# Tail stores of 64 rows dealt anew over the DMA engines, in the backward pass of a decode block with attention and a gated bilinear layer

## The chip, the core and the metric

The kernel runs on one core of one Trainium2 chip. The metric is device time in microseconds, from runs without the profiler. Beside those runs there is one profiled execution, with every instruction of the five compute engines and of SyncE (SP) and every packet of the DMA rings.

## The reference, cut to what matters

A block for a batch of 2 and one new token: layer norm, attention of 32 query heads on 16 cached key and value heads of 4,096 positions by 128, and a bilinear layer with gate, up and down weights. The kernel returns the output and the gradients for the input, both caches and all five weights, in bfloat16.

```python
def _B_ref(x, w_gate, w_up, w_down):
    g = jnp.einsum("bsd,df->bsf", x, w_gate)
    u = jnp.einsum("bsd,df->bsf", x, w_up)
    h = g * u
    return jnp.einsum("bsf,fd->bsd", h, w_down)

x = A_x
xn = _layernorm(x, axis=-1)
return x + _A_ref(xn, A_k_cache, A_v_cache, A_wq, A_wo) + _B_ref(xn, B_w_gate, B_w_up, B_w_down)
...
_out, _vjp = jax.vjp(_f, A_x, A_k_cache, A_v_cache, A_wq, A_wo, B_w_gate, B_w_up, B_w_down)
_grads = _vjp(grad_out)
```

What matters here are the gradients of `wq` (576 x 4096, out_4), of `w_gate` and of `w_up` (576 x 4608 each, out_6 and out_7). Each is an outer product: the transposed normalised input times a row of gradients, summed over the two batch entries. Of the 576 rows, 512 make four full blocks of 128; the other 64 are the tail. The tail of each matrix is stored in pieces of 64 rows by 512 columns, 64 KB each.

## The kernel before, in words

Nearly all the traffic is caches: 64 loads of 1 MB (key and value heads) and as many 1 MB stores of their gradients, with the weights and their gradients between them, 186 MB in all. Attention goes in 16 steps (8 groups of two key heads, times two batch entries). Nine pieces of the bilinear layer (`mlp(i, ...)`, i = 0 to 8, 512 hidden columns each) and the ends of the eight groups (`group_back(g)`, g = 0 to 7) are woven in.

The order of all work is written by a planner in the kernel, class `Order`, when the program is built. Each piece of work is a generator that yields its needs with their costs (`DVE(0.42)`, `ACQ("tl")`, `DMA("SP", ...)`), and the planner picks by due times (`PR`, `OFF`). What stands between two yields is emitted without a cost of its own. All large transfers are issued by SP on one ring.

Stores go through `put` (L695 to L700): wait for the pieces, issue the DMA on SP, and hand the buffer back once it has landed. The 64-row tails have buffers of their own, `tl` (two of them), and go through `tail_outer` (L818 to L843). The bilinear piece i stores two tails there, w = 0 for `w_gate` and w = 1 for `w_up`; a group stores one, for `wq`. The work of one tail is four matmuls on TensorE per column half (L831), one cast from PSUM to `tl` (`cp`, L470 on ACT or L472 on DVE), and the store (L699).

How a tail is spread over the sixteen DMA engines depends on how its destination is written. As `[64, 512]` it goes to sixteen engines, four rows each. Where the store's index is in `few` (L823), the destination is viewed with a leading dimension of four, `(r q) f -> q r f`, and it goes to four engines, sixteen rows each. Row p of the buffer then belongs to another row of the matrix, so that the weights on TensorE are taken from `xnq`, a copy of the last 64 columns of `xnr` in that order (made once by ACT at L637, in the tile `xi`, which is free by then).

Which tails go to four engines is set by `FEW_M` and `FEW_G` (L802): in bilinear pieces 0 to 4 only w = 1, in 5 to 8 both, and in groups 3 to 7. That is 18 tails on four engines and 8 on sixteen.

Of the kernel before, what the change touches and what calls it, by code (L numbers as in the profile page):

```python
# [13 lines left out]
P = 128  # L14


def view(t, p0, np_, off, dims):

    (pstep, _), *_ = t.ap
    return bass.AP(t.tensor, t.offset + p0 * pstep + off, [[pstep, np_], *[list(d) for d in dims]])  # L20
# [226 lines left out]
def PE(stream, issue=0.0, quad=None, kind="f"):  # L247
    return ("op", "PE", max(CLK * stream, issue) + 0.03, quad, stream, issue, kind)


def DVE(cost):
    return ("op", "DVE", cost)


def ACT(cost):
    return ("op", "ACT", cost)
# [10 lines left out]
def ACQ(tag):  # L267
    return ("acq", tag)


def REL(tag, i):
    return ("rel", tag, i)


def WAIT(*events):
    return ("wait", events)


def SET(event):
    return ("set", event)  # L280


def SPAWN(gen, prio):
    return ("spawn", gen, prio)


def PRIO(prio):
    return ("prio", prio)


def DMA(engine, cost, nbytes, row=8192):
    packet = 0.0364 * row + 8.7
    return ("dma", engine, cost, 0.02 + nbytes / 16e3 * packet / row, packet)
# [61 lines left out]
def kernel(  # L355
# [22 lines left out]
    nc = tc.nc  # L378
# [9 lines left out]
    NG = Hkv // G  # L388
# [8 lines left out]
    NFS = F // FS  # L397
# [61 lines left out]
    def events(n):  # L459
        return [Event() for _ in range(n)]  # L460
# [19 lines left out]
    xnr = const.tile([P, D], BF16, name="xnr")  # L480
    dyr = const.tile([P, D], BF16, name="dyr")

    def filled(name, shape, dtype, value, eng=nc.vector):
        t = const.tile(list(shape), dtype, name=name)
        eng.memset(t[:], value)
        return t
# [12 lines left out]
    xs = filled("xs", [P, 6, 32], BF16, 0.0)  # L499
    xi = const.tile([P, 2, P], BF16, name="xi")  # L500
    nc.vector.memset(xi[0:2], 0.0)
    xnq = xi[:, 0, 0:64]
    Wdy = filled("Wdy", [P, 2, 160], BF16, 0.0)

    for t in (*W_t[0], *W_t[1], *wm_t, *oT_t):
# [95 lines left out]
    def front():  # L601
        xb = xy[:, 0:D]
        yield DMA("ACT", 0.45, 2304, 1152)
        nc.scalar.dma_start(xb, A_x.rearrange("b s d -> (b s) d"))
        nc.scalar.dma_start(xy[:, D:2 * D], grad_out.rearrange("b s d -> (b s) d"))
        yield ("lset", Ein)
        yield ACT(1.5)
        nc.scalar.activation(warm[:], eps_t[0:1], AF.Sqrt)
        yield WAIT(Ein)
        yield DVE(1.0)  # L610
        for k in range(2):
            nc.vector.bn_stats(bst[:, k], xb[:, k * HD2:(k + 1) * HD2])
        nc.vector.bn_aggr(mv[:], bst[:].rearrange("p k s -> p (k s)"))
        yield ACT(0.3)
        nc.scalar.activation(rstd[:], mv[:, 1:2], AF.Sqrt, bias=eps_t[:], scale=1.0)
        yield DVE(0.6)
        nc.vector.reciprocal(rstd[:], rstd[:])
        nc.vector.tensor_scalar(xnb[:], xb, mv[:, 0:1], rstd[:], op0=ALU.subtract, op1=ALU.mult)
        yield ACT(1.5)
        nc.scalar.activation(warm[:], eps_t[0:1], AF.Exp)  # L620

        yield DVE(0.12)
        nc.vector.tensor_copy(view(xi[:], 0, 2, 0, [[P + 1, 2], [2, 64]]), view(xnb[:], 0, 2, 512, [[0, 2], [1, 64]]))
        i = yield ACQ("m")
        tp = m_t[i][:].bitcast(BF16)
        yield PE(0.02, 0.16)
        for c in range(4):
            nc.tensor.transpose(tp[:, 2 * c:2 * c + 2], xnb[:, c * P:(c + 1) * P], ident[0:2, 0:2])
        for h in range(2):
            nc.tensor.transpose(tp[:, 8 + 2 * h:10 + 2 * h], xi[0:2, h], ident[0:2, 0:2])  # L630
        yield DVE(0.16)
        nc.vector.tensor_copy(xs[:, :, 0:2], tp[:, 0:12].rearrange("p (c b) -> p c b", b=2))
        yield REL("m", i)
        yield SET(Exn)
        yield WAIT(Edy)
        yield from widen(xnb, xnr)
        nc.scalar.copy(xnq.rearrange("p (q r) -> p q r", q=4), xnr[:, 512:576].rearrange("p (r q) -> p q r", q=4))  # L637
        yield SET(Exr)

        yield PRIO(PR["const"])  # L640
        yield WAIT(Econst)
        nr = gg[0:2, 0, 0:4]
        yield DVE(0.3)
        nc.vector.memset(gg[:, 1], 0.0)
        nc.vector.tensor_scalar(nmu[:], mv[:, 0:1], -1.0, None, op0=ALU.mult)
        nc.vector.tensor_scalar(nr[:, 0:2], identf[0:2, 0:2], nmu[:], None, op0=ALU.mult)
        nc.vector.tensor_scalar(nr[:, 2:4], identf[0:2, 0:2], rstd[:], None, op0=ALU.mult)
        i = yield ACQ("m")
        tp, bp = m_t[i], m_t[i][:, 64:68]
        yield PE(0.0, 0.3)  # L650
        for a in range(4):
            for c in range(4):
                nc.tensor.matmul(tp[32 * c:32 * c + 32, 2 * a:2 * a + 2], lhsT=xb[:, P * c + 32 * a:P * c + 32 * a + 32],
                                 rhs=ident[0:2, 0:2], start=True, stop=True)
        for a in range(4):
            nc.tensor.matmul(tp[0:16, 8 + 2 * a:10 + 2 * a], lhsT=xb[:, 512 + 16 * a:528 + 16 * a],
                             rhs=ident[0:2, 0:2], start=True, stop=True)
        nc.tensor.matmul(bp, lhsT=view(ones[:], 0, 2, 0, [[0, P]]), rhs=nr, start=True, stop=True)
        yield DVE(0.9)
        nc.vector.tensor_copy(xnT[:, 0:8], tp[:, 0:8])  # L660
        nc.vector.tensor_copy(xnT[0:16, 8:16], tp[0:16, 8:16])
        nc.vector.tensor_copy(nrT[:], bp)
        for k, op in ((0, ALU.add), (2, ALU.mult)):
            nc.vector.tensor_tensor(xnT[:], xnT[:], view(nrT[:], 0, P, k, [[0, 8], [1, 2]]), op)
        nc.vector.memset(gg[:, 0], 0.0)
        yield REL("m", i)
        yield SET(Eprep)
# [131 lines left out]
                               out_4[0:512, gs[0] * FS:(gs[-1] + 1) * FS], p, E), p)  # L799
        yield SPAWN(release("Q", [grp[g]["Q"] for g in gs], [E]), p)  # L800

    FEW_M, FEW_G = (5, 6, 7, 8), range(3, NG)  # L802
    BUNCH = ((0, 1, 2, 3), (4, 5, 6, 7), (8,))
    Ds, dE = {}, [events(3) for _ in range(NFS)]

# [9 lines left out]
                yield SPAWN(cols_outer(rhss[0], dst, p, E[w]), p)  # L815
        yield SPAWN(release("D", [Ds[k] for k in ks], [*E, *[e for k in ks for e in dE[k][1:]]]), p)

    def tail_outer(rhss, dsts, p, event, w0=0, few=()):  # L818
        i = yield ACQ("tl")
        st = tl_t[i]  # L820
        nw, done = len(rhss), events(2)
        src = [st[64 * w:64 * w + 64, 0:FS] for w in range(w0, w0 + nw)]
        dsts = [d.rearrange("(r q) f -> q r f", q=4) if k in few else d for k, d in enumerate(dsts)]  # L823
        yield SPAWN(put(dsts, src, 64 * FS * 2, 1024, "tl", i, done), p + PR["store"])

        def mk(A):
            def mms(o):
                for w, rhs in enumerate(rhss, w0):
                    for aa in range(2):
                        a = 2 * A + aa  # L830
                        nc.tensor.matmul(o[64 * w:64 * w + 64, aa, 0:P],  # L831
                                         lhsT=(xnq[32 * a:32 * a + 32, :] if w - w0 in few else
                                               xnr[32 * a:32 * a + 32, 512:576]),
                                         rhs=rhs(a), start=True, stop=True)

            def ev(e, o):
                r = slice(64 * w0, 64 * (w0 + nw))
                cp(e, st[r, 256 * A:256 * A + 256].rearrange("p (a f) -> p a f", a=2), o[r, :, 0:P])
            return mms, (0.053, 0.104), 256, ev
        for A in range(2):  # L840
            yield SPAWN(unit(*mk(A), done[A]), p)
        yield WAIT(*done)
        yield SET(event)  # L843
# [12 lines left out]
    def mlp(i, hh, sl, Lgu, Ld, wd_slot):  # L856
# [12 lines left out]
        for w in range(2):  # L869
            for dc in range(5):  # L870
                for a in range(4):
                    if dc < 4:
                        k, rhs = dc, main[w][:, width * dc + FS * hh + P * a:width * dc + FS * hh + P * (a + 1)]
                    else:
                        h, big, c = at[a]
                        k, rhs = 4 + h, T[:, FT * w + c:FT * w + c + P] if big else gu[:, FS * w + c:FS * w + c + P]
# [16 lines left out]
        for k in range(NB):  # L893
            for e in range(2):
                nc.tensor.matmul(  # L895
                    dh, lhsT=Wdy[:, e, 2 * k:2 * k + P], rhs=view(X[:], 0, P, 64 * k + e, [[D, FC], [2, 32]]),
# [14 lines left out]
        po = pr("mlp", MLP_AT[i] / 4) + PR["wout"]  # L911
        yield SPAWN(rows_outer(hb[:], out_8[f0:f0 + FS, :], po, E[0]), po)
        yield SPAWN(tail_outer([lambda a, w=w: D2[32 * a:32 * a + 32, w, :] for w in range(2)],
                               [out[512:576, f0:f0 + FS] for out in (out_6, out_7)], po, dE[i][1],
                               few=(0, 1) if i in FEW_M else (1,)), po)
        for ks in BUNCH:
            if i == ks[-1]:
                yield SPAWN(grads(ks, po), po)
# [38 lines left out]
        for a in range(0, 4, n):  # L957
            _, big, c = at[a]
            t, step = (T, FT) if big else (gu, FS)
# [92 lines left out]
    def group_back(g):  # L1052
# [4 lines left out]
        r = yield ACQ("R")  # L1057
# [8 lines left out]
        for t, x in ((0, R), (1, Q)):  # L1066
# [4 lines left out]
        po = pr("back", 2 * g) + PR["wout"]  # L1071
# [1 line left out]
        t32(rT[:].rearrange("p c m -> p (c m)"), view(R[:], 0, P, 0, [[1, 4], [4, 32]]))  # L1073
        yield SPAWN(rows_outer(R[:], out_5[n0:n0 + FS, :], po, E[0]), po)
        yield SPAWN(tail_outer([lambda a: Q[32 * a:32 * a + 32, :]], [out_4[512:576, n0:n0 + FS]], po, E[1], g % 2,
                               few=(0,) if g in FEW_G else ()), po)
        if g == NG - 1:
            e = Event()
            yield SPAWN(cols_outer(lambda a: Q[32 * a:32 * a + 32, :], out_4[0:512, n0:n0 + FS], po, e), po)
# [20 lines left out]
        for be in range(4):  # L1100
            nc.tensor.matmul(view(rp, 0, P, 2 * be, [[8, GH], [1, 2]]),
                             lhsT=sel[:, be].rearrange("p a i -> p (a i)"), rhs=oT[:, 1, :, 0:2],
# [499 lines left out]
```

## Time and profile before

| | |
|---|---|
| median of 3 runs | 463.68 us (462.95 to 464.49) |
| the profiled execution's own time | 462.65 us |
| its span, first to last instruction | 460.7 us |
| mean granted TensorE clock | 0.721 |
| busy: PE, DVE, ACT, POOL | 80%, 79%, 73%, 31% |
| DMA packets and bytes | 40,494 and 185.97 MB, 404 GB/s |
| tail stores | 26 of 64 KB, issued from 47.1 to 451.3 us |

The span is the time between the first and the last instruction of the execution; the time of the execution has 1.95 us more around it. Busy time is an average over the whole span. In the slices of the page each digit is the busy share of one fortieth of the span, in tenths; the row for DMA is the mean of the sixteen engines. The packet records hold one line for each packet, with its start, length, bytes and ring. A DMA on one engine is a row of data packets and one 4-byte write that counts up the semaphore.

### The profile page before, as it was taken

To read this page: it belongs to the slowest core of one execution; us is meant where nothing else is said; L and a number is where in the kernel's file an instruction comes from. 1 tells how busy PE (TensorE), PEld (TensorE's weight loads), DVE (VectorE), ACT (ScalarE), POOL (GpSimd) and SP (SyncE) were. 2 spreads that over 40 slices of the span, in tenths; PEclk is the share of its full clock that TensorE was granted. 3 is DMA by queue.
4 is the path that set the end of the run, shared out by engine and by line. 5 is a ranking of instruction groups with operands and counts; after the bars stand their busy time and mean duration, and the time that the engine had idled before them with its cause. 6 is when DMAs were issued, how large, how long until landed. Compare 5 with 4: busy or idle time off the path is not lost.

```text
span 460.7 us, 15711 instructions
## 1 busy us (share of the span) xinstructions
PE 369.5 (80%) x6750; PEld 214.3 (47%) x6750; DVE 365.9 (79%) x708; ACT 336.8 (73%) x516; POOL 143.4 (31%) x174
## 2 busy tenths in 40 slices
PE   1688879798986786896978897877988887987994
PEld 1445456555443343554546364544444542544453
DVE  8887888896789687878887679886976987887782
ACT  4269638878986586775767859867867997897973
POOL 0740043403407341660016151050164364063000
PEclk9967676888776667757685678877567676675856
DMA  8999999999999999999999999999999999999995
GB/s 316 413 408 422 410 423 400 410 415 398 373 424 421 408 422 410 421 419 413 413 403 417 417 418 419 422 418 388 398 423 417 418 423 426 423 409 392 421 346 209
DMA packets 40494, 185.97 MB, mean 404 GB/s; under 512 B 3424, under 2 KB 12136, under 8 KB 24040
## 3 DMA queue, kind: packets, MB, share of 16 engines
q1 hardware_dynamic: 40416, 184.96, 99.0%
q8 instruction: 53, 0.87, 0.7%
q14 instruction: 17, 0.14, 0.1%
q10 hardware_dynamic: 8, 0.00, 0.0%
HBM read 92.48 MB, written 92.48 MB: 401 GB/s over the span
## 4 chain that ended last, share of the span: by engine, by line
DMA 34%; PE 30%; ACT 14%; DVE 12%; issue 5%; SPq 3%; DVEq 0%; ACTq 0%
DMA big<-in_A_v_cache_dram 15%; DMA out_dram<-big 14%; ACT big L470 12%; DVE big L466 7%; PE ps_o L1299 5%; PE ps_m L1451 4%; PE ps_o L730 4%; PE ps_m L1277 4%; DMA big<-in_A_k_cache_dram 3%; SPq L1201 2%; PE ps_o L767 2%; DVE big L472 2%; PE ps_m L895 2%; PE ps_m L681 2%; DMA ww<-in_A_wq_dram 1%
## 5 line engine op out<-in xcount | busy, mean ns | idle before, releaser
L470 ACT CAST big<-ps_o 128x1024 bf16<-128x1024 f32 (+2 forms) x309 | 278.9, 964 | 49.8 <-PE ps_o L1299 24.3
L466 DVE STREAM_TRANSPOSE big<-big 128x1024 f32<-128x1024 f32 x146 | 176.3, 1222 | 16.1 <-DMA big<-in_A_v_cache_dram 6.3
L1265 POOL TENSOR_TENSOR BD<-vr,mask 128x2048 bf16<-128x2048 bf16 x32 | 115.3, 3604 | 114.3 <-DVE vr L472 45.4
L472 DVE CAST big<-ps_o 128x1024 bf16<-128x1024 f32 (+1 forms) x69 | 73.4, 1065 | 19.4 <-PE ps_o L767 6.1
L1277 PE MATMUL ps_m<-big,W 128*32 128x128 bf16 x2048 | 59.7, 280 | 4.5 <-issue 1.7
L1242 POOL COPY W<-rep 32x16 bf16<-32x16 bf16 x128 | 24.8, 193 | 117.9 <-DVE rep L1015 102.0
L1277 PEld LDWEIGHTS <-W 128*32 128x32 bf16 x2048 | 47.2, 125 | 25.1 <-issue 23.9
L1299 PE MATMUL ps_o<-BD,dd 32*128 32x512 bf16 x256 | 46.9, 497 | 9.1 <-ACT big L470 8.1
L1299 PE MATMUL ps_o<-BD,pp 32*128 32x512 bf16 x256 | 44.6, 473 | 8.9 <-ACT big L470 7.3
L466 DVE STREAM_TRANSPOSE big<-ww 128x1152 f32<-128x1152 f32 (+1 forms) x25 | 32.9, 1318 | 2.6 <-DMA out_dram<-big 2.5
L1451 PE MATMUL ps_m<-big,pp 128*32 128x512 bf16 x256 | 28.9, 540 | 4.1 <-DVE pp L466 2.4
L1451 PE MATMUL ps_m<-big,dd 128*32 128x512 bf16 x256 | 27.8, 528 | 1.7 <-DVE dd L466 0.6
L1299 PEld LDWEIGHTS <-dd 32*128 32x128 bf16 x256 | 11.2, 98 | 26.5 <-issue 20.0
L1299 PEld LDWEIGHTS <-pp 32*128 32x128 bf16 x256 | 10.3, 95 | 28.1 <-issue 24.5
L767 PEld LDWEIGHTS <-xnr 32*128 32x128 bf16 x368 | 13.1, 114 | 14.5 <-issue 13.1
L730 PE MATMUL ps_o<-dyr,R 32*32 32x288 bf16 x256 | 17.8, 401 | 1.2 <-ACT big L470 1.1
L767 PE MATMUL ps_o<-D,xnr 32*128 32x128 bf16 x256 | 13.9, 265 | 5.7 <-ACT big L470 4.3
L730 PE MATMUL ps_o<-dyr,hb 32*32 32x288 bf16 x288 | 15.7, 328 | 2.8 <-ACT big L470 2.7
L1047 POOL COPY qr<-qd 128x256 bf16<-128x256 bf16 x8 | 3.2, 398 | 47.4 <-DVE qd L472 43.2
L895 PE MATMUL ps_m<-big,Wdy 128*128 128x128 bf16 x162 | 16.7, 285 | 0.6 <-DVE cr L1403 0.5
L895 PEld LDWEIGHTS <-Wdy 128*128 128x128 bf16 x162 | 15.1, 131 | 2.9 <-issue 2.7
L1352 ACT COPY mr<-m 1x128 f32<-1x128 f32 x16 | 4.7, 295 | 15.1 <-DVE m L1350 14.9
(210 smaller groups left out, 488.2 us busy)
## 6 DMA issues: line engine op xcount, KB each, us to landing
out_dram<-big SPq DMA_DIRECT2D x74, 1024.0 KB
big<-in_A_k_cache_dram SPq DMA_DIRECT2D x32, 1024.0 KB
big<-in_A_v_cache_dram SPq DMA_DIRECT2D x32, 1024.0 KB
out_dram<-big SPq DMA_DIRECT2D x17, 576.0 KB
ww<-in_B_w_down_dram SPq DMA_DIRECT2D x9, 576.0 KB
ww<-in_A_wo_dram SPq DMA_DIRECT2D x8, 576.0 KB
ww<-in_A_wq_dram SPq DMA_DIRECT2D x8, 512.0 KB
big<-in_B_w_gate_dram SPq DMA_DIRECT2D x4, 1024.0 KB
```

Of the source, the lines that this page charges most:

```text
L466: nc.vector.transpose(out, in_)
L470: nc.scalar.copy(out, in_)
L472: nc.vector.tensor_copy(out=out, in_=in_)
L681: nc.tensor.matmul(dp[32 * q:32 * q + 32, 0:P], lhsT=W, rhs=view(X, 0, P, xoff(q, s), [[FS, 4], [2, 32]]), start=(s == 0), stop=(s == S - 1))
L730: nc.tensor.matmul(o[32 * q:32 * q + 32, aa, 0:HD2], lhsT=view(t, 32 * q, 32, 2 * A + aa, [[4, 32]]), rhs=dyr[32 * q:32 * q + 32, k * HD2: ...
L767: nc.tensor.matmul(o[:, aa, j * P:(j + 1) * P], lhsT=xnr[32 * a:32 * a + 32, dc * P:(dc + 1) * P], rhs=rhs(a), start=True, stop=True)
L895: nc.tensor.matmul(dh, lhsT=Wdy[:, e, 2 * k:2 * k + P], rhs=view(X[:], 0, P, 64 * k + e, [[D, FC], [2, 32]]), start=(k == 0 and e == 0), s ...
L1242: nc.gpsimd.tensor_copy(view(W_t[t][w][:], 32 * a, 32, 6 + 8 * a, [[G * WW, 4], [WW, G], [1, 2]]), view(rep_t[grp[g]["qs"]][:], 32 * a, 32 ...
L1265: nc.gpsimd.tensor_tensor(BD_t[i][:], view(vr_t[v][:], 0, P, 0, [[0, 16], [1, Dh]]), view(mask16[:], 0, P, 0, [[1, 16], [0, Dh]]), ALU.mult)
L1277: nc.tensor.matmul(sc[32 * cq:32 * cq + 32, :], lhsT=view(W[:], 0, P, (be * G + l) * WW + 6 - 4 * c2 - 2 * l, [[1, 32]]), rhs=view(X[:], 0 ...
L1299: nc.tensor.matmul(o[:, k, :], lhsT=pr2[32 * c4:32 * c4 + 32, :], rhs=BD[32 * c4:32 * c4 + 32, 8 * l + 4 * h2:8 * l + 4 * h2 + 4, :], star ...
L1451: nc.tensor.matmul(ct[32 * j:32 * j + 32, :], lhsT=view(rT, 0, P, 4 * c + 2 * l, [[1, 32]]), rhs=kv_t[kvS[s][t][l]][:, Dh * c:Dh * (c + 4) ...
```

## The change

`few` is now a table from the store's index to the number of engines, four or two. Two permuted copies of the 64 columns are made in `xi` instead of one: the second takes the other half of row 0 of the tile, and one more copy on ACT. The tables deal the tails anew:

- from four engines to two: w = 1 of pieces 0, 1, 2 and 3, w = 0 of piece 8, and the tail of group 7 (six);
- from sixteen engines to four: w = 0 of piece 4, and the tails of groups 1 and 2 (three).

After it 5 tails go to sixteen engines, 15 to four and 6 to two. On every engine the instructions stand in the same order as before.

```diff
-    xnq = xi[:, 0, 0:64]
+    xnq = {4: xi[:, 0, 0:64], 2: xi[:, 0, 64:P]}
...
-        nc.scalar.copy(xnq.rearrange("p (q r) -> p q r", q=4), xnr[:, 512:576].rearrange("p (r q) -> p q r", q=4))
+        for q, t in xnq.items():
+            nc.scalar.copy(t.rearrange("p (q r) -> p q r", q=q), xnr[:, 512:576].rearrange("p (r q) -> p q r", q=q))
...
-    FEW_M, FEW_G = (5, 6, 7, 8), range(3, NG)
+    FEW_M = {0: {1: 2}, 1: {1: 2}, 2: {1: 2}, 3: {1: 2}, **{i: {0: 4, 1: 4} for i in range(4, NFS - 1)}, NFS - 1: {0: 2, 1: 4}}
+    FEW_G = {0: 0, **{g: 4 for g in range(1, NG - 1)}, NG - 1: 2}
...
-        dsts = [d.rearrange("(r q) f -> q r f", q=4) if k in few else d for k, d in enumerate(dsts)]
+        dsts = [d.rearrange("(r q) f -> q r f", q=few[k]) if k in few else d for k, d in enumerate(dsts)]
...
-                                         lhsT=(xnq[32 * a:32 * a + 32, :] if w - w0 in few else
+                                         lhsT=(xnq[few[w - w0]][32 * a:32 * a + 32, :] if w - w0 in few else
...
-                               few=(0, 1) if i in FEW_M else (1,)), po)
+                               few=FEW_M[i]), po)
...
-                               few=(0,) if g in FEW_G else ()), po)
+                               few={0: FEW_G[g]} if FEW_G[g] else {}), po)
```

More of the change, by code (lines that the diff above doesn't have):

```diff
@@ L816, in grads, with tail_outer @@
         yield SPAWN(release("D", [Ds[k] for k in ks], [*E, *[e for k in ks for e in dE[k][1:]]]), p)
-    def tail_outer(rhss, dsts, p, event, w0=0, few=()):
+    def tail_outer(rhss, dsts, p, event, w0=0, few={}):
         i = yield ACQ("tl")
```

## The prediction

> **What bounds the kernel now.** I read the page's slices and queue table first, then the instructions on tile `tl`, then SP's waits and the end of its timeline, and last the single packet records of the trace.
>
> ```profile
> DMA  8999999999999999999999999999999999999995
> ...
> DMA packets 40494, 185.97 MB, mean 404 GB/s; under 512 B 3424, under 2 KB 12136, under 8 KB 24040
> ...
> q1 hardware_dynamic: 40416, 184.96, 99.0%
> ```
>
> The sixteen DMA engines are busy in every slice but the last, and one ring (q1, SP's) holds 99.0% of their time; no compute engine is above 80%. The bound is DMA engine time. SP itself waits 86.7 us for ACT and 63.9 us for DVE, but ahead of a full ring.
>
> The small packets tell the dealing. 201 transfers run on all sixteen engines, each engine closing with one 4-byte semaphore write: 3,216. The tail stores add 18 x 4 + 8 x 16 = 200, the two small output stores 2 x 2, the two small loads on ACT's ring as much: 3,424, the page's count. So a `q=4` tail does run on four engines. After the change it should be 3,424 - 200 + (5 x 16 + 15 x 4 + 6 x 2) = 3,376.
>
> ```profile
> L699 SPq DMA_DIRECT2D out_dram<-tl x26: 472/558/3377, 47.1 to 451.3; - x26
> L470 ACT CAST tl<-ps_o x25: 353/370/440, 46.6 to 450.9; 128x256 bf16<-128x256 f32 x13, 64x256 bf16<-64x256 f32 x12
> ```
>
> Twenty-six tail stores; SP spends about half a microsecond on each.
>
> A mean over engines hides the question, which is who finishes last. The packet records carry start, length, bytes and ring, no engine number; but on one engine the next packet starts 3 to 4 ns before the last one ends, so chains can be followed. A run of sixteen 1,024-byte packets and a semaphore write is a four-engine tail on one of its engines. When the four engines enter it (us from the span's start):
>
> ```
> tail store of      four engines enter it at         last behind first
> mlp 0              52.08   52.12   52.74   53.67     1.6
> mlp 3              112.68  113.05  113.38  116.59    3.9
> mlp 4              224.84  224.92  225.35  230.06    5.2
> mlp 6, first       281.86  281.94  282.30  287.10    5.2
> group 5            361.51  361.63  364.21  367.29    5.8
> group 6            405.41  405.69  408.56  411.77    6.4
> mlp 8, first       440.93  441.81  443.07  446.30    5.4
> ```
>
> So the four are far from alike. One, call it X, is always last. Which is it? The small output store of two rows goes to two engines; its rows start at 451.37 and 452.06, while X ends the transfer before it at 455.95. X is not one of those two.
>
> ```profile
> 449.70 0.27 SPq L1495 DMA_DIRECT2D out_dram<-xy  x1
> 450.85 0.35 SPq L699 DMA_DIRECT2D out_dram<-big  x1
> 451.31 1.08 SPq L699 DMA_DIRECT2D out_dram<-tl  x1
> 453.47 0.38 SPq L699 DMA_DIRECT2D out_dram<-big  x1
> 456.59 0.26 SPq L1495 DMA_DIRECT2D out_dram<-xy  x1
> ```
>
> This is the end of SP's queue. The ring runs on after it: the last packet is X's, at 459.40 of the 460.7 span. The two engines of the small store are A (unimportant: it leads and runs dry after 444) and B, whose chain from the tail at 443.07 to the row at 452.06 has no gap; B is through with the last big store at 455.55, 3.85 us before X. One more laggard, Y, belongs to the twelve engines without tails: it leaves the row store before mlp 8's tail at 448.15 (X 446.30, all others by 443.15) and ends at 459.03, 0.37 before X. On X each transfer was issued 1.4 to 15.9 us before its turn, so X works without a pause; its own work is the span.
>
> No record here names an engine. The Trainium skill ("DMA: Bandwidth & Descriptors", section on why a DMA increments its semaphore by 16) says that a DMA from SP runs on the lowest-numbered k engines, k being the largest number up to 16 that divides both outer dimensions; by that A and B are engines 0 and 1, and X is 2 or 3.
>
> **The change, part by part.** Prices, from the same chains: sixteen packets and the semaphore write, entry to entry, 0.684 us; four, 0.176; thirty-two (read from the 1,024-byte column stores at the end), 1.361.
>
> - Six tails from four engines to two (mlp 0 to 3, one of mlp 8's, group 7): A and B each +1.361 - 0.684 = +0.677, six times +4.06. X and its neighbour each lose 0.684, six times -4.10.
> - Three tails from sixteen to four (group 1, mlp 4's first, group 2): A, B, X and its neighbour +0.684 - 0.176 = +0.508, three times +1.52; the twelve others -0.176, three times -0.53.
> - Net: A and B +5.59 (2.71 of it before 117 us, 1.35 after 440), X and its neighbour -2.58, Y and the rest -0.53.
> - One more copy on ACT, 128x64, at the start: 0.25 us as the one at 10.92, and ACT then sits idle 0.70 until 11.87. Covered; uncovered it would cost 0.25 once.
> - The order of instructions on all five queues is the same in both kernels; the matmuls of nine tails merely take their weights from another place. No wait is added.
> - SP's issue of a two-engine tail is not shown. The row of all tails gives 0.47 to 0.76 us for nearly every one, so 0 to +0.3 each; with 1.4 us of queue ahead at the worst, hidden, hence 0.
>
> Each engine runs at its own pace, so the end is the latest of four sums (packet end in this profile):
> X 459.40 - 2.58 = 456.8. Y 459.03 - 0.53 = 458.5. A would be near 458.6. B: 455.55 + 5.59 = 461.1, less what it spends waiting anyway. It does so once: between 117.3 and 119.6 the 4,096-byte packets of a store issued late show 305 ns instead of 159, since the ring is being filled while they run. The four-engine tail before it was left at 113.36 to 114.07; two stores of 2.49 would end at 118.3 to 119.0, the first engines end at 119.36. So 0.3 to 1.0 us of B's first +2.71 falls into that hole. I take 0.7 (B is one of three close engines): B ends at 460.45, **1.05 us after X did**.
>
> The profiled execution took 462.65 us (span 460.7, 1.95 around it); the sum gives 463.7. The median of the three runs is 463.68, 1.03 above the profiled one; with the same 1.05 added it becomes **464.7 us**. A measurement of this kernel can tell about 0.3% (1.4 us) from no change, so the likeliest is a change inside that bound, on the slow side.
>
> **Rivals.**
>
> *B's lead is smaller than in this profile: slower.* B's lead over X is 1.6 at 52 us and only 3.2 at 443; every engine meets stalls of its own (packets of 700 to 1,200 ns where 309 is usual, and instruction fetches of 0.65 us, X's every 73 us). The change takes 5.59 + 2.58 = 8.2 us from a lead of at most 5.4. With no hole at 117 and one more 0.9 us stall on B the end is 459.40 + (5.59 - 3.85) + 0.9, that is 2.6 us later: 466.3. It decides once B is held over 0.4 us more than I take. For it: even here B comes out last. The Trainium skill's rules for kernel authors (same page, "Rules for kernel authors", use all 16 engines) speak against the change too: an outer dimension below 16 confines the whole DMA to that many engines. By that rule alone, with no lead to eat up, all 5.59 us would be added: 469.3. The table above speaks against that full sum.
>
> *X alone holds the kernel: faster.* If in most runs X is a microsecond further behind (the median is 1.03 above this execution) and B as far ahead as A, X's 2.58 us come off whole: 461.1. For it: X is last of its four in every row. Against it: Y ends only 0.37 us before X and gains 0.53, so in this execution nothing better than 0.9 is open.
>
> *Y is last, and B stays clear: no change that can be told.* Y's 458.5 is 0.9 before the old end: 462.8.
>
> *The two-dimensional store does not land on two engines, or not on those of the small store.* Then six of the moves fall elsewhere; against it stands the count 3,424 that works out exactly, so I give it no share of its own.
>
> **How the numbers follow.** B last but within the bound 0.30, Y last 0.12: together same 0.42. B last by more than the bound: 0.40, because two of the three unknowns (the hole, a stall on B) push that way. X alone: faster 0.18. The range for 8 in 10 runs from a little above the faster rival's 461.1, 462.2, to the slower rival's end, 466.4. Within the forecast alone (0.3 to 1.0 us for the hole) it is 464.4 to 465.1.
>
> **What would show it.** The count of packets under 512 B at 3,376 (packets in all 40,446). Six tails with thirty-two 1,024-byte packets in a row, 1.36 us, on two engines each, the two that also carry the rows of the small store. X and B about level at mlp 6's first tail, where X is 4.8 us behind now, and B the last of the four from about 320 us on. The last packet of the execution on B, some 1 us later than 459.40. I am wrong if the last packet is X's or Y's, if q1's queue runs dry for long stretches (then the order of transfers moved, not only their dealing), or if B's extra packets vanish in pauses that I have not seen.

## The result, and the profile after

The changed kernel takes 467.16 us (median of 5 runs, 465.76 to 468.34), the kernel before 463.80 us (5 runs, 462.95 to 464.49): a ratio of 1.0071, with a 95% interval of 1.0046 to 1.0097. It is slower by 3.3 us (2.1 to 4.5). The forecast was 464.7, with a range up to 466.4; the time lies above it.

The profiled execution of the changed kernel took 467.67 us, 5.0 more than that of before. These are two single executions, one 0.5 above the median of its kernel and one 1.15 below: 1.7 of the 5.0 is the choice of executions.

The page of the changed kernel, its slices and queue table:

```profile
DMA  8999999999999999999999999999999999999995
...
DMA packets 40446, 185.97 MB, mean 399 GB/s; under 512 B 3376, under 2 KB 12088, under 8 KB 23992
...
q1 hardware_dynamic: 40368, 184.96, 98.7%
```

The dealing is what the diff says: 3,376 small packets and 40,446 in all, both as worked out ahead. The engines are busy in the same slices as before, and at first sight nothing is lost. The instructions on tile `tl`:

```profile
L700 SPq DMA_DIRECT2D out_dram<-tl x26: 482/564/2838, 48.0 to 456.0; - x26
L470 ACT CAST tl<-ps_o x25: 357/372/445, 47.4 to 455.4; 128x256 bf16<-128x256 f32 x13, 64x256 bf16<-64x256 f32 x12
```

SP's issues and ACT's casts cost what they did (median 564 ns against 558, 372 against 370); the last tail is merely issued 4.7 us later. The end of SP's queue:

```profile
453.86 0.27 SPq L1497 DMA_DIRECT2D out_dram<-xy  x1
455.24 0.35 SPq L700 DMA_DIRECT2D out_dram<-big  x1
456.03 0.71 SPq L700 DMA_DIRECT2D out_dram<-tl  x1
458.76 0.39 SPq L700 DMA_DIRECT2D out_dram<-big  x1
461.73 0.26 SPq L1497 DMA_DIRECT2D out_dram<-xy  x1
```

The issue at the head of this list stood at 449.70 before, the one at its end at 456.59: SP itself is 4 to 5 us late. Behind it the ring ends on B. From the packet records of the changed kernel (us from the span's start):

```
B   row of the small store            460.30
B   group 7's tail, 32 packets        461.75 to 463.12
B   last big store, 32 packets        463.11 to 464.48
B   row of the last small store       464.48 to 464.53   the last packet
Y   ends                              462.58
A   row of the small store            457.60
most engines leave the last 1 MB store at 456.6 to 457.4; before, at 451.4 to 452.0
```

So B is last, as forecast, with two-engine tail, big store and row in one unbroken chain. But Y, which has three tails less, also ends 3.55 us later than its 459.03 of before, and so do the engines that are never last. Where did the others lose it? Three stretches of the execution (length; busy time of PE, PEld, DVE, ACT and POOL; then the clock, the DMA share and GB/s), first before, then changed:

```profile
120.00:230.00 110.00, 88.30 (x1562) 49.71 (x1551) 88.73 (x161) 78.65 (x120) 37.22 (x50) 0.70 1.02 414
230.00:260.00 30.00, 24.94 (x521) 15.57 (x519) 25.26 (x47) 22.32 (x33) 9.15 (x11) 0.68 1.02 411
260.00:440.00 180.00, 151.94 (x2617) 83.58 (x2615) 142.36 (x254) 145.55 (x221) 60.63 (x65) 0.71 1.01 415
```

```profile
120.00:230.00 110.00, 87.34 (x1602) 48.87 (x1595) 88.97 (x160) 80.91 (x123) 38.44 (x51) 0.72 1.01 411
230.00:260.00 30.00, 21.33 (x482) 13.96 (x484) 22.35 (x43) 18.71 (x29) 9.14 (x11) 0.66 1.00 380
260.00:440.00 180.00, 154.59 (x2580) 82.35 (x2578) 142.61 (x255) 145.55 (x219) 60.56 (x65) 0.69 1.01 412
```

The DMA share hides it; the GB/s show it. Between 230 and 260 us the changed kernel moves 380 instead of 411: 0.9 MB less, or 2.3 us at that rate. The stretch ahead of it lacks 0.8 us and the one behind it 1.3. This is rough, since the stretches stand still while the work moves by up to 5 us. SP's queue at that place, before and changed:

```profile
222.80 2.07 SPq L699 DMA_DIRECT2D out_dram<-tl  x2
...
234.27 1.20 SPq L1194 DMA_DIRECT2D big<-in_B_w_up_dram  x1
235.57 6.81 SPq L1152 DMA_DIRECT2D big<-in_A_k_cache_dram  x2
242.47 0.52 SPq L1179 DMA_DIRECT2D ww<-in_A_wo_dram  x1
```

```profile
224.88 4.75 SPq L700 DMA_DIRECT2D out_dram<-tl  x2
...
238.53 1.15 SPq L1196 DMA_DIRECT2D big<-in_B_w_up_dram  x1
239.77 7.37 SPq L1154 DMA_DIRECT2D big<-in_A_k_cache_dram  x2
247.23 0.38 SPq L1181 DMA_DIRECT2D ww<-in_A_wo_dram  x1
```

The issue of mlp 5's two tails, at 224.88, is 2.1 us later than before and takes 4.75 us, from the start of the first to the end of the second, instead of 2.07: this is the larger step. The two key loads keep SP for 7.37 us instead of 6.81, where an issue normally takes 0.3 to 0.6. They start 4.2 us later, and 4 to 5 us late the stream stays to the end. All sixteen engines added up, from the packet records:

```
us, summed over 16 engines                before   changed
16 x end of the last packet                7350      7432
packets at their usual length (1)          6996      6996
what packets took beyond it                 167       227
instruction fetches                          59        61
no packet recorded                          128       148
(1) 309 ns for 8,192 bytes, 178 for 4,608, 46 for 1,024, and so on, each less
    the 3 to 4 ns by which packets of one engine overlap
```

The work is the same to the last microsecond. The 82 us more (16 x 5.1) are packets that took longer (60) and pauses (20). Fourteen of the engines had less to do than before, and ended late all the same.

### The profile page after: what moved, and what is told of

The parts are those of the page before. It is cut to its first block, busy times and chain, and to the rows that moved or that the text cites. A ratio compares the mean times of both kernels' runs of the same rounds, so it can differ in the third digit from the quotient of the medians.

```text
span 465.9 us, 15712 instructions
## 1 busy us (share of the span) xinstructions
PE 372.5 (80%) x6750; PEld 212.3 (46%) x6750; DVE 366.0 (79%) x708; ACT 337.4 (72%) x517; POOL 143.1 (31%) x174
## 2 busy tenths in 40 slices
DMA packets 40446, 185.97 MB, mean 399 GB/s; under 512 B 3376, under 2 KB 12088, under 8 KB 23992
## 5 line engine op out<-in xcount | busy, mean ns | idle before, releaser
L1279 PE MATMUL ps_m<-big,W 128*32 128x128 bf16 x2048 | 57.5, 273 | 3.2 <-issue 1.0
L1279 PEld LDWEIGHTS <-W 128*32 128x32 bf16 x2048 | 45.7, 122 | 23.7 <-issue 22.5
L1301 PE MATMUL ps_o<-BD,pp 32*128 32x512 bf16 x256 | 46.5, 483 | 7.9 <-ACT big L470 6.5
L1453 PE MATMUL ps_m<-big,dd 128*32 128x512 bf16 x256 | 28.9, 546 | 2.5 <-DVE dd L466 1.9
L897 PEld LDWEIGHTS <-Wdy 128*128 128x128 bf16 x162 | 14.1, 125 | 3.3 <-issue 3.0
```

The source lines that it names most:

```text
L897: nc.tensor.matmul(dh, lhsT=Wdy[:, e, 2 * k:2 * k + P], rhs=view(X[:], 0, P, 64 * k + e, [[D, FC], [2, 32]]), start=(k == 0 and e == 0), s ...
L1279: nc.tensor.matmul(sc[32 * cq:32 * cq + 32, :], lhsT=view(W[:], 0, P, (be * G + l) * WW + 6 - 4 * c2 - 2 * l, [[1, 32]]), rhs=view(X[:], 0 ...
L1301: nc.tensor.matmul(o[:, k, :], lhsT=pr2[32 * c4:32 * c4 + 32, :], rhs=BD[32 * c4:32 * c4 + 32, 8 * l + 4 * h2:8 * l + 4 * h2 + 4, :], star ...
L1453: nc.tensor.matmul(ct[32 * j:32 * j + 32, :], lhsT=view(rT, 0, P, 4 * c + 2 * l, [[1, 32]]), rhs=kv_t[kvS[s][t][l]][:, Dh * c:Dh * (c + 4) ...
```

## The experiments

Each kernel is the changed one with other tables `FEW_M` and `FEW_G` (the engines per tail), so each carries the second copy on ACT. The diffs are cut to these tables; a minus line is the old dealing, as in the first kernel, and in the last one the line of the changed kernel. Ratios are to the kernel before, with 95% intervals; the us behind a ratio are what it adds to 463.6. A sum "with 4.55 in hand" is the prediction's: X ends at 459.40, Y at 459.03, B at 455.55 - 0.7, plus what is dealt to each. "In hand" is what B can take before it ends last.

**The copy alone** (old dealing).

```diff
+    FEW_M = {i: {0: 4, 1: 4} if i > 4 else {1: 4} for i in range(NFS)}
+    FEW_G = {g: 4 if g > 2 else 0 for g in range(NG)}
```

> The tails are dealt as before; only the second permuted copy on ACT is there. Every theory: 463.8 us, within 0.3% of before, since ACT sat idle 0.70 us behind that copy. If it is slower by 1 us or more, the copy at the start moves the whole order of arrivals, and what the changed kernel lost is not due to the dealing.

463.42 us, ratio 1.0010 (0.9997 to 1.0023): the copy costs nothing that can be told. This run gives something else besides, a second execution with the old dealing to look into. Its small store's rows start at 451.21 and 452.81, the last packet ends at 459.28. With 0.05 for the row, 1.41 for the row store, 0.69 for the tail and 1.36 for the big store B would have been through at 456.3: **3.0 us in hand, where the execution of the prediction had 3.85.**

**The four early moves from four engines to two.**

```diff
-    FEW_M = {i: {0: 4, 1: 4} if i > 4 else {1: 4} for i in range(NFS)}
+    FEW_M = {i: {0: 4, 1: 4} if i > 4 else {1: 2 if i < 4 else 4} for i in range(NFS)}
```

> Only the four early moves from four engines to two (mlp 0 to 3). Theory 1, the prediction's sum with B's whole lead of 3.85 us: B 455.55 + 2.71 - 0.7 = 457.6, X 456.7, Y stays at 459.03, so 0.4 us less than before, 463.4 us, same. Theory 2, no lead counts and what is dealt to the two engines is paid in full: +2.7, 466.5 us. Theory 3, B's lead counts only where the work is added: at mlp 3 the two engines are 3.2 to 3.5 us ahead of X, three moves (2.03) and a stall use that up, and the fourth (0.68) is paid: +0 to +0.7, 463.8 to 464.5 us, and B, not X, is the last of the four from mlp 4 on.

464.14 us, 1.0022 (1.0009 to 1.0034): +1.0 us. Neither the sum with all of B's lead (-0.4) nor the full price (+2.7); theory 3 (0 to +0.7) comes nearest. In its trace B ends at 461.67, 0.3 before the last.

**The three moves from sixteen to four.**

```diff
-    FEW_M = {i: {0: 4, 1: 4} if i > 4 else {1: 4} for i in range(NFS)}
-    FEW_G = {g: 4 if g > 2 else 0 for g in range(NG)}
+    FEW_M = {i: {0: 4, 1: 4} if i > 3 else {1: 4} for i in range(NFS)}
+    FEW_G = {g: 4 if g > 0 else 0 for g in range(NG)}
```

> Only the three moves from sixteen engines to four (groups 1 and 2, mlp 4's first). X is last of its four and takes 3 x 0.508 = 1.52 us more, the twelve others 0.53 less. Theories 1 to 3 alike: X ends at 460.9, +1.5, 465.3 us. If the time stays at 463.8, the lag of X is made up elsewhere (its stalls, or waits that it would have had anyway).

465.71 us, 1.0061 (1.0044 to 1.0078): +2.8 us, or 2.4 by the medians, with X last at 462.17. More than the 1.5 of the packets.

**The two late moves from four to two.**

```diff
-    FEW_M = {i: {0: 4, 1: 4} if i > 4 else {1: 4} for i in range(NFS)}
-    FEW_G = {g: 4 if g > 2 else 0 for g in range(NG)}
+    FEW_M = {i: {0: 2 if i == NFS - 1 else 4, 1: 4} if i > 4 else {1: 4} for i in range(NFS)}
+    FEW_G = {g: (2 if g == NG - 1 else 4) if g > 2 else 0 for g in range(NG)}
```

> Only the two late moves from four engines to two (mlp 8's first tail and group 7's). Theory 1 and theory 3: B 455.55 + 1.35 = 456.9, X 458.0, Y 459.03, so 0.4 us less, 463.4 us, same. Theory 2 (paid in full): +1.35, 465.2 us.

463.12 us, 0.9993 (0.9980 to 1.0006): no difference. 1.35 us more on B cost nothing, so some lead there is.

**Which of the three moves?** First mlp 4's alone, then those of groups 1 and 2 alone.

```diff
+    FEW_M = {i: {0: 4, 1: 4} if i > 3 else {1: 4} for i in range(NFS)}     # first kernel
+    FEW_G = {g: 4 if g > 0 else 0 for g in range(NG)}                      # second kernel
```

> Only one of the three moves from sixteen engines to four: mlp 4's first tail, which then stands in a bunch of four four-engine tails (217 to 225 us). Theory P (X, the last of the four, paces the ring, and each such move costs its 0.508 us, or somewhat more, wherever it is): +0.5 to +0.9, about 464.1 us. Theory Q (the bunch is what costs: SP is held longer at the end of it, 6.7 instead of 5.6 us at the next key load, and the other engines run short of work): nearly all of the three moves' +2.4 is here, 465 us or more.

464.60 us, 1.0022 (1.0007 to 1.0036): +1.0 us.

> Only the other two moves from sixteen engines to four: the tails of groups 1 and 2, each alone in its stretch. Theory P: +1.0 to +1.7, about 464.8 us. Theory Q: +1.0 at the most, and no longer hold of SP at 235 us than before.

464.74 us, 1.0018 (1.0006 to 1.0029): +0.8 us. There is no single costly place (theory Q falls): SP's first load at the place named there takes 5.63 us with mlp 4's move alone and 5.60 with the other two, as before. Together the parts come to 1.8, near the packets' 1.5.

**The reverse: mlp 5's tails on sixteen, and all tails on sixteen.**

```diff
+    FEW_M = {i: {} if i == 5 else {0: 4, 1: 4} if i > 4 else {1: 4} for i in range(NFS)}   # mlp 5
+    FEW_M, FEW_G = {i: {} for i in range(NFS)}, {g: 0 for g in range(NG)}                  # all
```

> The reverse, on the kernel before: both tails of mlp 5 go from four engines to sixteen. X has 1.02 us less, the twelve others 0.35 more. By the engines' sums alone Y ends at 459.38 and X at 458.4, no gain, 463.4 us. Theory P (the pacing engine's work counts, about once and a half): -0.4 to -1.5. Theory Q: -1 or better, with SP held less than 5.6 us at the key load behind.

463.22 us, 0.9992 (0.9972 to 1.0011): no gain, as the engines' sums say, since Y then is last.

> All 26 tails on sixteen engines: X and its neighbours have 18 x 0.508 = 9.1 us less, the twelve others, Y among them, 3.17 more. By the sums Y ends at 459.03 + 3.17 = 462.2: +2.8, 466.2 us. If the lag of the last engine is what costs, whichever engine it is, and the lag of Y behind the rest of the twelve is smaller than X's was, less than that: 463 to 465 us. A faster kernel here would mean that the dealing on four engines is itself what costs.

466.58 us, 1.0062 (1.0044 to 1.0079): +2.9 us, where the sum for Y says +2.8. The page counts what that dealing must give, 3,424 + 18 x 12 = 3,640 small packets:

```profile
DMA packets 40710, 185.97 MB, mean 401 GB/s; under 512 B 3640, under 2 KB 12352, under 8 KB 24256
```

Relieving four engines by 9.1 us is worth nothing while one of the twelve others has 3.2 more. The Trainium skill ("DMA: Bandwidth & Descriptors", section "Rules for kernel authors") asks for transfers that use all 16 engines; here the runs decide against it for these 64-row stores, in this order of the other transfers.

**All six moves to two engines, none of the three.**

```diff
+    FEW_M = {i: {0: 2 if i == NFS - 1 else 4, 1: 4} if i > 4 else {1: 2 if i < 4 else 4} for i in range(NFS)}
+    FEW_G = {g: (2 if g == NG - 1 else 4) if g > 2 else 0 for g in range(NG)}
```

> All six moves of the change from four engines to two, none of the three from sixteen to four. The two engines have 4.06 us more, X and its neighbour 4.10 less. Theory S (the prediction's sum: B may take 3.85 + 0.7 = 4.55 us before it shows): Y stays last, -0.4 us, 463.3. Theory L (B has only some 2.3 us in hand, which is what the changed kernel's +3.3 says: 5.59 - 3.3): +1.8, 465.4. Theory A (each part costs what it cost alone, 1.0 for the early four and -0.3 for the late two): +0.7, 464.3. With no lead: +4.1, 467.7.

464.29 us, 1.0020 (1.0006 to 1.0033): +0.9 us (0.3 to 1.5). Its trace shows B last. SP's final issue stands at 457.94:

```profile
455.02 0.39 SPq L700 DMA_DIRECT2D out_dram<-big  x1
457.94 0.26 SPq L1497 DMA_DIRECT2D out_dram<-xy  x1
```

A's row of that store starts at 458.67, at once; B's at 460.62, and that is the last packet (460.68). So the step "Y is last" is wrong here: B is. Against B in the kernel with the copy alone (when B leaves the row store ahead of the tail, us):

```
                      copy alone   six moves   later by   dealt until then
ahead of mlp 4          225.96      229.88       3.92        2.71
ahead of mlp 7          307.13      311.17       4.04        2.71
group 6                 408.68      411.98       3.30        2.71
ahead of mlp 8          443.81      446.49       2.68        2.71
end (first worked out)  456.3       460.68       4.4         4.06
```

B's extra time is what was dealt to it, and up to 1.3 us more that comes and goes. Nothing of it was absorbed at 117 us. With the copy alone, the two nearly equal engines of which B is one leave mlp 3's tail at 115.12 and 115.15 and the two stores behind it at 120.10 and 120.13: 4.98 us, the time of two stores without a slow packet. With the six moves B leaves that tail at 117.69 and the two stores at 122.67: again 4.98. In neither trace is there a hole that B could have filled.

**Six moves again, but all after 280 us.**

```diff
+    FEW_M = {i: {0: 2 if i > 5 else 4, 1: 2 if i in (6, 7) else 4} if i > 4 else {1: 4} for i in range(NFS)}
+    FEW_G = {g: (2 if g == NG - 1 else 4) if g > 2 else 0 for g in range(NG)}
```

> Six moves from four engines to two again, but all after 280 us: both tails of mlp 6 and 7, mlp 8's first and group 7's. The sums of every engine are those of the six of the change. Theory S: -0.4, 463.3 us. Theory L: +1.8, 465.4. If the place counts (a lead is there late and not early, since late moves alone cost nothing): 463.3 to 463.7, clearly below the six of the change.

465.59 us, 1.0035 (1.0019 to 1.0052): +1.6 us. Late moves are no cheaper than early ones (1.6 against 0.9, with intervals that overlap), so the place isn't the reason. In hand were 4.06 - 1.6 = 2.4 us.

**All 18 four-engine tails to two.**

```diff
+    FEW_M = {i: {0: 2, 1: 2} if i > 4 else {1: 2} for i in range(NFS)}
+    FEW_G = {g: 2 if g > 2 else 0 for g in range(NG)}
```

> A large dose: all 18 tails that run on four engines go to two. The two engines have 18 x 0.677 = 12.2 us more, and so must be last. What is missing from 12.2 is what B has in hand. Theory S: 12.2 - 4.55 = +7.6, 471.3 us. Theory L: +9.9, 473.5. With no lead: +12.2, 475.8. More than 12.2: the stores on two engines cost something besides their packets (SP's issue, buffers held longer).

474.27 us, 1.0225 (1.0207 to 1.0243): +10.4 us (9.6 to 11.3), so 1.8 in hand (0.9 to 2.6). The prediction's 4.55 is excluded, for stores that cost their packets and nothing else. B ends last at 471.92, A at 471.42. Now the page shows idle engines too, the q1 share falling from 99.0% and single slices to 8:

```profile
DMA  8999999999999999999999998989999999999985
...
q1 hardware_dynamic: 40380, 184.96, 97.5%
```

**A try at a faster kernel**: the two late moves, and mlp 5's tails on sixteen.

```diff
+    FEW_M = {i: {} if i == 5 else {0: 2 if i == NFS - 1 else 4, 1: 4} if i > 4 else {1: 4} for i in range(NFS)}
+    FEW_G = {g: (2 if g == NG - 1 else 4) if g > 2 else 0 for g in range(NG)}
```

> A try at a faster kernel: the two late moves from four to two, and mlp 5's tails from four to sixteen. X has 1.37 + 1.02 = 2.39 us less, B 1.35 - 1.02 = 0.33 more, Y and the other eleven 0.35 more. By the sums Y is last at 459.38: no change, 463.6 us. If each part brings what it brought alone (-0.3 and -0.4): 462.9.

463.62 us, 1.0005 (0.9990 to 1.0021): no change, as the sums say. With X, Y and B within four microseconds of each other, no dealing tried here beats the kernel before.

**Does a move from sixteen to four cost more than its packets?** The three had cost 2.4 to 2.8 for 1.5, and on top of the six again 3.3 - 0.9 = 2.4.

```diff
+    FEW_M, FEW_G = {i: {0: 4, 1: 4} for i in range(NFS)}, {g: 4 for g in range(NG)}              # all 26 on four
+    FEW_M = {i: {0: 2 if i == NFS - 1 else 4, 1: 2 if i < 4 else 4} for i in range(NFS)}         # and the six on two
+    FEW_G = {g: 2 if g == NG - 1 else 4 for g in range(NG)}
```

> All eight tails that run on sixteen engines go to four (26 on four): X, its neighbour and the two lowest have 8 x 0.508 = 4.06 us more, the other twelve 1.41 less. Theory S (packets only, and X is last): +4.1, 467.7 us. Theory R (a move from sixteen to four costs about 1.6 times its packets, as the three seem to: +2.4 for 1.52): +6.5, 470.1 us.

468.19 us, 1.0094 (1.0068 to 1.0119): +4.4 us (3.2 to 5.5). The packets' 4.1 fits; 1.6 times that is excluded.

> The changed kernel with the other five sixteen-engine tails on four as well: the two lowest engines have 4.06 + 4.06 = 8.1 us more, X and its neighbour as much as before, the twelve others 1.41 less. With 2.4 us in hand for B, as the six late moves and the large dose show: Theory S +5.7, 469.3 us. Theory R: six moves alone +0.9, and 6.5 for the eight: +7.4, 471.0 us.

469.13 us, 1.0119 (1.0090 to 1.0148): +5.5 us (4.2 to 6.9); 8.1 less 2.4 in hand is 5.7. B is last again, at 466.82.

**The eight on eight engines.**

```diff
-    xnq = {4: xi[:, 0, 0:64], 2: xi[:, 0, 64:P]}
+    xnq = {4: xi[:, 0, 0:64], 8: xi[:, 0, 64:P]}
...
+    FEW_M = {i: {0: 4 if i > 4 else 8, 1: 4} for i in range(NFS)}
+    FEW_G = {g: 4 if g > 2 else 8 for g in range(NG)}
```

> The eight tails on sixteen engines go to eight: eight packets and a semaphore write (0.346 us, from 16 x 0.0424 = 0.678 and 4 x 0.0424 = 0.170 about halfway) for 0.176 on eight engines, X among them: 8 x 0.17 = +1.4 us; the other eight have 1.4 less. Theory S: X last, +1.4, 465.0 us. Theory R: +2.2, 465.8.

466.26 us, 1.0049 (1.0027 to 1.0071): +2.3 us (1.3 to 3.3). It tells nothing apart: 1.4 and 2.2 both lie inside.

The sums against the runs, in us against the kernel before:

```
kernel                         last by the sum    4.55 in hand   2.4 in hand   measured
changed kernel                 B                      +1.05          +3.2      +3.3 (2.1 to 4.5)
early four to two              Y; B                   -0.4           +0.3      +1.0 (0.4 to 1.6)
late two to two                Y                      -0.4           -0.4      -0.3 (-0.9 to 0.3)
six to two                     Y; B                   -0.4           +1.7      +0.9 (0.3 to 1.5)
six to two, late               Y; B                   -0.4           +1.7      +1.6 (0.9 to 2.4)
18 to two                      B                      +7.6           +9.8     +10.4 (9.6 to 11.3)
six to two, eight to four      B                      +3.6           +5.7      +5.5 (4.2 to 6.9)
three to four                  X                      +1.5           +1.5      +2.8 (2.0 to 3.6)
eight to four                  X                      +4.1           +4.1      +4.4 (3.2 to 5.5)
mlp 4's first to four          X                      +0.5           +0.5      +1.0 (0.3 to 1.7)
groups 1 and 2 to four         X                      +1.0           +1.0      +0.8 (0.3 to 1.3)
eight to eight                 X                      +1.4           +1.4      +2.3 (1.3 to 3.3)
mlp 5 to sixteen               Y                       0.0            0.0      -0.4 (-1.3 to 0.5)
late two, mlp 5 to sixteen     Y                       0.0            0.0      +0.2 (-0.5 to 1.0)
all on sixteen                 Y                      +2.8           +2.8      +2.9 (2.0 to 3.7)
```

For the six late moves the prediction's own sum is rather +0.2, since the 0.7 of the hole at 117 us lies ahead of them.

The number 2.4 was taken from the changed kernel and the six late moves; the kernel with the six and the eight, and the 18 moves, bear it out. Three rows lie outside their interval: the early four (measured 0.7 above the sum), the six (0.8 below) and the three (1.3 above).

The numbers fit another reading as well. With 3.0 in hand, as in the copy-alone trace, and 0.06 us for each two-engine store on top of its packets, the six kernels in which the sums put B last or nearly so (changed, early four, six, six late, 18, six and eight) come to +3.0, 0.0, +1.4, +1.4, +10.3 and +5.5. No run tells less in hand from a small extra cost per store.

## Why the prediction was wrong, point by point

*The bound, and who carries which tail: right.* The counts of packets came out exactly. The two engines with the two-engine tails are those of the small store: tail, big store and row form one chain on B.

*B last of the four, and the last packet on B: right, and earlier than said.* At mlp 6's first tail the four stand at 286.37, 288.11, 289.02 and 291.53. There "X and B about level" was forecast, and B last from about 320. The last of them is B, already at group 3 (264.50, the others up to 261.99).

*"The last packet some 1 us later than 459.40": wrong; it was 464.53.* **The step that failed is "B ends at 460.45", that is, the lead of 3.85 and the 0.7 us of the hole that were taken off the 5.59 dealt to B.** The prices of the tails and the sum of 5.59 hold: the large doses rise by them. What was mis-sized is what B had in hand: 2.4 us (1.7 to 3.1 by the single runs) instead of 4.55, if a two-engine store costs its packets and nothing else. Of the 2.15 us between the two:

- The hole at 117 us, 0.7 us, gave nothing: two traces show this. With the copy alone and with the six moves B passes that place in 4.98 us, without a slow packet. SP's issues from 112 to 124 us stand within 0.2 us of the old ones in the kernel with the six, so they did not move the place away. In the trace of the prediction B, as third of the four, waited there 0.3 us at least; that wait belonged to the one execution.
- The lead of 3.85 came from one execution too, and a second one with the same dealing had 3.0. But 3.85 over the last engine was no outlier. In five more traces X and B got the same extra work, and the same working gives 3.8 (the three), 2.6 (mlp 4's), 4.5 (the groups'), 3.1 (the eight to four) and 4.3 (the eight to eight). The mean of the seven is 3.6, so the lead explains about 0.25.
- About 1.2 us has no cause shown. B loses more than its packets once work is added to it, or each two-engine store costs a little more than its packets.

The reading "B is through with the last big store at 455.55" is a sum too, and not what the trace of before shows. SP issued that store at 453.47, its first packet on any engine stands at 454.40, and the first engine is through at 455.86. B waited there, and 455.55 is where it would have been without that wait. As what B could still take on, the 3.85 stands.

The rival "B's lead is smaller" came nearest, at 466.3. Its terms, no hole and 0.9 us more of stalls on B, are close to what the traces show; the lead itself it left at 3.85. With 2.4 in place of those terms it is 459.40 + 3.2 and, to the median, 467.0, but 2.4 was taken in part from this very kernel.

*"Each engine runs at its own pace": wrong for the others.* Y was forecast at 458.5 and ended at 462.58; most engines left the last 1 MB store 5 us later than before, with 0.5 us less dealt to them. What they lost stands in the records as slow packets and pauses. That an engine can run only so far ahead of the last one, since one SP queue feeds all, and that the loss passes through SP's held issues and through buffers that come free late, is argued from the rows above; no run here takes the one away without the other.

*What stays open.* The three moves from sixteen to four cost 2.8 us (2.0 to 3.6) on the kernel before, 1.3 over their packets, though their parts alone sum to 1.8 and eight such moves to 4.4. It may be a chance meeting of stalls in this one dealing; nothing here shows it. On top of the six moves, too, they cost 2.4 (3.3 - 0.9), about a microsecond over their packets.

*The copy on ACT and SP's issue: right,* nothing for the one, and a median of 564 ns against 558 for the other.

## What to carry to other kernels

Where sixteen engines carry one stream, count what an edit adds to each engine and look for the one that ends last: fourteen of the fifteen sums above came within 1 us of the measurement once the starting gap was known. Take that gap, what an engine can bear before it is last, from a dose large enough to turn the order round: seven traces told leads of 2.6 to 4.5 us where the doses found 2.4. And don't stack moves on two engines that lead by only three or four microseconds: the relief of the others is lost as soon as one of the two becomes last.

## What the runs showed of the hardware

A packet that takes longer counts in full as a busy engine. In the changed kernel the DMA share is 1.00 in the stretch that moves 380 GB/s and 1.02 where before moves 411; only GB/s and the lengths of the packets (227 us beyond the usual over the whole execution, against 167) tell.

Engines with equal work end several microseconds apart, and part of it is instruction fetches on the same engines. From 215 us on, as far as the chains can be followed, that of Y in the trace of before holds five fetches of 16 KB, each with a pause of 0.86 to 1.05 us and up to 0.5 of slow packet; X's holds one of these and four of 8 KB, with a pause of 0.30 and about 0.35 more; B's holds none of the first kind and three of the second. B's 8 KB fetches stand at 218.0, 300.8 and 378.4 us, and at nearly the same times with the copy alone (217.3, 300.7, 377.9) and with the six moves (217.9, 301.2, 378.3): that is how B can be known again in another trace.
